# A linear-attention and channel-mix kernel: the layout of transposed q, where batch 0 is divided, and a new order of the work

## The chip, the cores and the metric

One core of one Trainium2 chip runs the whole program. The metric is device time in microseconds (us) of one execution; a verdict compares medians of several executions. A core has TensorE (matmuls, PE in the profile; PEld is its loading of weights), VectorE (DVE), ScalarE (ACT), GpSimd (POOL) and SyncE (SP). POOL and SP issue the DMAs here.

## What is computed

There are 8 batches, 8 heads, 576 tokens and 64 values a head; the model width C is 512 and the hidden width F is 1024. The reference, cut to its core:

```python
kv  = einsum('bhsd,bhse->bhde', k, v)             # 64x64 per head, no softmax
out = einsum('bhsd,bhde->bhse', q, kv)            # called u below
out = out / sqrt(mean(out*out, -1) + 1e-6) * g_norm
x   = out with the heads side by side: (8, 576, 512)
xp  = x moved down by one token (zero first)
xk  = mu_k*x + (1-mu_k)*xp;  xr = mu_r*x + (1-mu_r)*xp
kk  = maximum(xk @ w_k, 0);  vv = (kk*kk) @ w_v;  r = 1/(1+exp(-(xr @ w_r)))
result = r * vv
```

## The kernel before

**Attention, by batch.** q, k and v come in as bf16, by DMAs that POOL issues (in the order of the `ld` pieces); of batch 0, half of k and of v come as fp32 by SP (`ldh`) and are cast on the chip (`cst`). With the heads in two groups z = 0 and 1, the pieces of batch b are, by name and line:
- `kv` (L265): the 64x64 products of k and v, 72 matmuls for all heads; `kc` copies them from PSUM, `ks` (L271) parts even and odd rows with a permutation matrix, `kd` copies them back to SBUF as `kv`.
- `tq` (L350): VectorE transposes q in blocks of 32x32 fp32 words, each word being two neighbouring bf16 values of a head. A partition of the loaded q holds 36 tokens (QJ) of 1/16 (QP) of a head, so a block turns one token of 32 partitions. Two pieces a batch (four for batch 0, which goes by head group), 18 in all. The result is `qT`: a partition holds a pair of the 64 values, and along it lie the tokens of two heads (e = 0 and 1), two bf16 (r = 0 and 1) each. Word number: 36 times the source partition plus the token in it, so that tokens lie in their order and a transpose writes words 36 apart.
- `u` (L281): kv times qT. A piece covers half of the tokens (i = 0 or 1) of the heads. For r = 0, then r = 1, it runs one matmul for each pair of heads m and each e, of 32 rows and 64 columns; the eight of one r sit in different places of the array.
- `uc` (scale by g_norm, to SBUF), `sq` (squares), `ss` (a matmul that sums squares by head), `rs` (1/sqrt), `sp` (batches 2 and later: SP's DMAs spread rs over the partitions, L418), `mul`, `d` (difference to the token before, L298), `mk`/`mr` (times mu-1), `xk`/`xr` (sum, L311).

**Channel mix, by groups of 512 rows.** `k` (L494, group 0: L470) is xk times w_k in PSUM, `relu` (L453) and `ksq` (square, L504) bring it to SBUF, `r` (L516) and `sig` are the gate, `v` (L536) is the product with w_v, `out` (L549) multiplies it with the gate, `st` stores it. Group g needs batches g-1 and g; group 0's `k0.<half><i><z>` uses 256 rows of batch 0 and head group z.

**Batch 0** is cut more finely, by head group and by token parts: columns 0 to 256 and 256 to 576 (`PARTS`, with GA = 256), while the other batches are cut at 288 (HS). In a name such as `xk0.01`, the last digits are head group and part.

**PSUM** holds four tiles `ps` of two banks each. A piece that takes a tile waits until the readers of its last content are done.

**The order.** Nothing is scheduled by a program: the string `ORDER` lists all pieces, and each engine runs its own in that order, so an engine that waits holds up all that it has behind. `@A` and `@D` put a piece that can run on either on ScalarE or VectorE. `z:512` is a matmul on zeros that fills TensorE before k0.000; its result is overwritten.

Of the kernel before, what the change touches and what calls it, by code (L numbers as in the profile page):

```python
# [7 lines left out]
FP32 = mybir.dt.float32  # L8
BF16 = mybir.dt.bfloat16
# [47 lines left out]
def kernel(  # L57
# [13 lines left out]
    nc = tc.nc  # L71

    B, H, S, HD = q.shape
# [5 lines left out]
    NZ = NHP // 2  # L79
    HS = S // 2  # L80
    QP = 16
# [9 lines left out]

    const = ctx.enter_context(tc.tile_pool(name="const", bufs=1))
    sb = ctx.enter_context(tc.tile_pool(name="sb", bufs=2))
    psum = ctx.enter_context(tc.tile_pool(name="psum", bufs=2, space=bass.MemoryType.PSUM))
    ctx.enter_context(tc.manual_schedule())

    BUFS = {
        "k": (3, (128, NHP, NJ * HD), BF16),
        "v": (3, (128, NHP, NJ * HD), BF16),
        "q": (3, (128, QJ * HD), BF16),  # L100
        "kv": (2, (128, 2, 2 * HD), BF16),
        "kvn": (2, (128, 2, 2 * HD), BF16),
        "qT": (2, (128, 2 * S, 2), BF16),
        "uT": (4, (128, 2, S), BF16),
        "sq": (3, (128, 2, S), BF16),
        "rs": (3, (128, 2, S), BF16),
        "rsc": (1, (128, S), BF16),
        "d": (2, (128, 2, S), BF16),
        "md": (4, (128, 2, S), BF16),
        "sqk": (2, (128, NFC, G), BF16),  # L110
        "relu": (3, (128, 2, G), BF16),
        "sig": (3, (128, 2, C), BF16),
        "out": (3, (128, 2, C), FP32),
        "ps": (4, (128, 2, 512), FP32),
    }
# [158 lines left out]
    def u_tiles(pss, kv, qT, zs, c0, c1):  # L274
        for r in range(2):
            for z in zs:
                for y in range(2):
                    for e in range(2):
                        m = 2 * z + y
                        rows_ = slice(32 * m, 32 * m + 32)  # L280
                        nc.tensor.matmul(pss[z][64 * e:64 * e + 64, y, 0:c1 - c0], kv[rows_, r, HD * e:HD * e + HD],  # L281
                                         qT[rows_, S * e + c0:S * e + c1, r], start=(r == 0), stop=(r == 1))
# [9 lines left out]
    def blends(b, z, name, x0, w, deps, mds, dd):  # L292
# [9 lines left out]
        for key, dst, m0 in (("k", xk, 0), ("r", xr, NHP)):  # L302
            md = mds[key]

            def mul(eng, md=md, m0=m0):
                for y in range(2):
                    hp = m0 + 2 * z + y
                    scale(eng, get(md)[:, y, cs], dd.t[:, y, cs], cols[:, hp:hp + 1])

            def plus(_, md=md, dst=dst):  # L310
                nc.vector.tensor_tensor(out=dst[:, 2 * z:2 * z + 2, r0:r0 + w], in0=md.t[:, :, cs], in1=xT[:, :, cur],  # L311
                                        op=ALU.add)

            m = add(f"m{key}" + name, "DA", mul, deps=[df, p_cols], bufs=[dd, md])
            done[key] = add(f"x{key}" + name, "D", plus, deps=[m] + x_free.get((b - RB, key), []),
                            bufs=[md, x_buf[(b, z)]])
        return done

    PARTS = ((0, GA), (GA, S))

    def parts(b):
        return PARTS if b == 0 else ((0, HS), (HS, S))

    def attention(b):
        kin, vin, qin = (kvq[(m, b)] for m in ("k", "v", "q"))
        kv, qT = Buf("kv"), Buf("qT")
        bufs = [{t: Buf(t) for t in ("uT", "sq", "rs", "d")} for z in range(NZ)]
        mds = [{"k": Buf("md"), "r": Buf("md")} for z in range(NZ)]
        x_ready[b] = {"k": [], "r": []}
        zss = [[0], [1]] if b == 0 else [[0, 1]]  # L330
        qd, kvcs = {}, {}
        for zs in zss:
# [12 lines left out]
            for i in range(2):  # L345
                def tq(_, i=i, part=part):
                    src = qin.t.bitcast(FP32).rearrange("q (j i) -> q j i", i=32)
                    dst = get(qT).rearrange("q t r -> q (t r)").bitcast(FP32).rearrange("q (p j) -> q j p", j=QJ)
                    js = slice(QJ // 2 * i, QJ // 2 * i + QJ // 2)
                    nc.vector.transpose(out=dst[part, js, :], in_=src[part, js, :])  # L350

                ts.append(add(f"tq{name}.{i}", "D", tq, deps=sum((loaded[("q", b, z)] for z in zs), []), bufs=[qin, qT]))
# [4 lines left out]
        for i, (c0, c1) in enumerate(parts(b)):  # L357
            for zs in zss:
                p = add(f"u{b}." + "".join(map(str, zs)) + f".{i}", "T", lambda _, zs=zs, i=i, c0=c0, c1=c1: u_tiles(
                    {z: get(us[z][i]) for z in zs}, kv.t, qT.t, zs, c0, c1),  # L360
                    deps=sum(([*qd[z], kvcs[z]] for z in zs), []), bufs=[us[z][i] for z in zs] + [qT, kv])
                for z in zs:
                    pu[(z, i)] = p
        secs = {}
        for z in range(NZ):
            for i, (c0, c1) in enumerate(parts(b)):
                name, ps, w, cs = f"{b}.{z}{i}", us[z][i], c1 - c0, slice(c0, c1)
                uT, sq = bufs[z]["uT"], bufs[z]["sq"]
                uc = add("uc" + name, "DA", lambda eng, ps=ps, uT=uT, cs=cs, w=w: scale(
# [235 lines left out]
```

## Time and profile before

| | us |
|---|---|
| median of 3 runs | 202.54 (202.31 to 202.99) |
| the profiled execution | 202.8 |
| its span, first to last instruction | 201.0 |
| TensorE busy in the span | 189.8 |
| VectorE busy | 138.3 |
| ScalarE busy | 129.5 |
| the 18 transposes, together | 21.3 |

The span is the part of the execution that has instructions in it; 1.8 us of the execution lie around it. Busy times of engines overlap. The granted clock of TensorE is 1.00 over the whole span. A busy TensorE includes the fillers, 37 of which are recorded with 12.4 us.

### The profile page before, as it was taken

The page shows a single profiled execution, that of the slowest core. Times are in us where ns is not written, and L with a number is a line of the kernel's source. Part 1 is how long each engine was busy: PE and PEld are TensorE (multiplying, and loading weights), DVE is VectorE, ACT ScalarE, POOL GpSimd, SP SyncE. Part 2 cuts the span into 40 slices and gives each one's busy share as a digit, 9 for nine tenths or more (in the row PEclk, how much of TensorE's full clock was granted, in tenths as well). Part 3 has the DMA queues.
Part 4 walks back from the last instruction along what each step waited for, and adds up shares of the span by engine and source line. Part 5 has one row for each costly group of instructions (what it writes and reads, how often), then busy time and mean ns, then how long its engine had stood idle before and what let it go on. Part 6 is the DMA issues. An engine that isn't in the chain of part 4 may idle for free.

```text
span 201.0 us, 4245 instructions
## 1 busy us (share of the span) xinstructions
PE 189.8 (94%) x1743; PEld 93.9 (47%) x1765; DVE 138.3 (69%) x229; ACT 129.5 (64%) x172; POOL 23.1 (12%) x41
## 2 busy tenths in 40 slices
PE   7999779988999999999999999999999999999992
PEld 2545664443544444544545754444444444444451
DVE  1596687997879999797897798998454423133252
ACT  2367978957998579898968689375963554312500
POOL 7743331212100500000000000000000000000000
PEclk9999999999999999999999999999999999999999
DMA  6999999999999999999614242551000202045044
GB/s 212 198 210 216 201 206 216 203 207 219 207 230 257 246 250 265 238 213 194 230 26 94 105 124 50 165 163 57 0 0 0 104 3 104 0 157 209 0 151 166
DMA packets 21016, 30.63 MB, mean 152 GB/s; under 512 B 1917, under 2 KB 14469, under 8 KB 20997
## 3 DMA queue, kind: packets, MB, share of 16 engines
q0 software_dynamic: 11264, 16.19, 45.1%
q1 hardware_dynamic: 9588, 14.03, 21.9%
q8 instruction: 14, 0.23, 0.4%
q10 hardware_dynamic: 144, 0.13, 0.2%
q14 instruction: 6, 0.04, 0.1%
HBM read 33.56 MB, written 9.44 MB: 214 GB/s over the span
## 4 chain that ended last, share of the span: by engine, by line
PE 73%; DMA 9%; DVE 8%; ACT 4%; issue 2%; POOL 2%; SPq 1%; POOLq 0%; DVEq 0%
PE ps L536 27%; PE ps L494 26%; PE ps L516 12%; DMA w_k<-in_moe_w_k_dram 6%; DMA rs<-rsc 3%; PE ps L281 2%; DVE out L549 2%; DVE qT L350 2%; PE ps L470 1%; PE ps L265 1%; ACT relu L453 1%; ACT md L134 1%; DVE xk L311 1%; SPq L418 1%; PE ps L380 1%
## 5 line engine op out<-in xcount | busy, mean ns | idle before, releaser
L536 PE MATMUL ps<-w_v,sqk 128*128 128x512 bf16 (+1 forms) x286 | 65.8, 373 | 0.8 <-issue 0.3
L494 PE MATMUL ps<-xk,w_k 128*128 128x512 bf16 (+1 forms) x282 | 58.2, 355 | 0.7 <-issue 0.3
L453 ACT ACTIVATE relu<-ps 128x1024 bf16<-128x1024 f32 x36 | 36.2, 1022 | 27.9 <-PE ps L494 27.5
L536 PEld LDWEIGHTS <-sqk 128*128 128x128 bf16 x296 | 28.0, 98 | 32.8 <-issue 2.4
L494 PEld LDWEIGHTS <-w_k 128*128 128x128 bf16 x288 | 27.7, 98 | 27.5 <-issue 1.5
L504 DVE TENSOR_TENSOR sqk<-relu 128x1024 bf16<-128x1024 bf16 x32 | 21.6, 687 | 21.5 <-ACT relu L453 21.4
L516 PE MATMUL ps<-w_r,xr 128*128 128x512 bf16 x140 | 33.2, 379 | 0.2
L549 DVE TENSOR_TENSOR out<-ps,sig 128x1024 f32<-128x1024 f32 x16 | 19.5, 1220 | 11.5 <-PE ps L536 7.3
L371 ACT ACTIVATE sq<-ps 128x576 bf16<-128x576 f32 (+2 forms) x32 | 20.3, 650 | 9.1 <-PE ps L281 8.0
L526 ACT ACTIVATE sig<-ps 128x1024 bf16<-128x1024 f32 x18 | 18.3, 1022 | 8.5 <-PE ps L516 7.8
L350 DVE STREAM_TRANSPOSE qT<-q 128x576 f32<-128x576 f32 (+1 forms) x18 | 21.3, 1201 | 2.5 <-DMA q<-in_q_dram 2.1
L516 PEld LDWEIGHTS <-xr 128*128 128x128 bf16 x144 | 13.9, 98 | 16.6 <-issue 0.5
L134 ACT ACTIVATE md<-d,cols 128x576 bf16<-128x576 bf16 (+2 forms) x26 | 16.7, 698 | 0.5 <-DVE d L298 0.5
L144 ACT ACT_TABLE_LOAD x12 | 15.4, 1283 | 0.9 <-PEq L589 0.7
L136 DVE TENSOR_SCALAR uT<-ps,cols 128x576 bf16<-128x576 f32 (+1 forms) x16 | 12.5, 801 | 4.4 <-PE ps L281 2.2
L393 DVE TENSOR_TENSOR xT<-uT,rs 128x1152 bf16<-128x1152 bf16 (+2 forms) x18 | 12.3, 685 | 3.6 <-ACT rs L286 3.5
L311 DVE TENSOR_TENSOR xk<-md,xT 128x1152 bf16<-128x1152 bf16 (+2 forms) x18 | 12.2, 687 | 3.4 <-ACT md L134 3.2
L136 DVE TENSOR_SCALAR md<-d,cols 128x576 bf16<-128x576 bf16 (+2 forms) x46 | 13.9, 354 | 0.2
L438 PE MATMUL ps<-zero 128*128 128x512 bf16 x37 | 12.4, 477 | 1.5 <-DVE zero L164 1.2
L298 DVE TENSOR_TENSOR d<-xT 128x1152 bf16<-128x1152 bf16 (+2 forms) x18 | 12.5, 692 | 0.5
L311 DVE TENSOR_TENSOR xr<-md,xT 128x1152 bf16<-128x1152 bf16 (+2 forms) x18 | 12.1, 683 | 0.7 <-ACT md L134 0.6
L134 ACT ACTIVATE uT<-ps,cols 128x576 bf16<-128x576 f32 (+2 forms) x16 | 11.9, 743 | 0.6 <-PE ps L281 0.6
(47 smaller groups left out, 105.9 us busy)
## 6 DMA issues: line engine op xcount, KB each, us to landing
out_dram<-out SPq DMA_DIRECT2D x35, 256.0 KB, 2.4
q<-in_q_dram POOLq DMA_DIRECT2D x7, 576.0 KB, 21.4
v<-in_v_dram POOLq DMA_DIRECT2D x6, 576.0 KB, 21.9
k<-in_k_dram POOLq DMA_DIRECT2D x6, 576.0 KB, 20.5
rs<-rsc SPq DMA_DIRECT2D x48, 72.0 KB, 2.8
w_k<-in_moe_w_k_dram POOLq DMA_DIRECT2D x2, 512.0 KB, 11.3
w_v<-in_moe_w_v_dram POOLq DMA_DIRECT2D x2, 512.0 KB, 16.1
k<-in_k_dram POOLq DMA_DIRECT2D x3, 288.0 KB, 12.8
```

The source lines that it names most:

```text
L134: nc.scalar.mul(out=dst, in_=src, mul=col)
L136: nc.vector.tensor_scalar(out=dst, in0=src, scalar1=col, scalar2=None, op0=ALU.mult)
L311: nc.vector.tensor_tensor(out=dst[:, 2 * z:2 * z + 2, r0:r0 + w], in0=md.t[:, :, cs], in1=xT[:, :, cur], op=ALU.add)
L350: nc.vector.transpose(out=dst[part, js, :], in_=src[part, js, :])
L371: sq_ = add("sq" + name, "A", lambda _, ps=ps, sq=sq, cs=cs, w=w: nc.scalar.activation(out=get(sq)[:, :, cs], in_=ps.t[:, :, 0:w], func=AF ...
L453: nc.scalar.activation(out=get(rt), in_=ps.t, func=AF.Relu)
L494: nc.tensor.matmul(get(ps)[:, fc % 2, a0:a1], w_k_sb[:, cc, 128 * fc:128 * fc + 128], xk[:, cc, x0:x0 + a1 - a0], start=(cc == 0), stop=(c ...
L504: nc.vector.tensor_mul(out=get(sqk)[:, 2 * f2:2 * f2 + 2, :], in0=rt.t, in1=rt.t)
L516: nc.tensor.matmul(get(ps)[:, ci % 2, :], xr[:, cc, n0:n0 + 128], w_r_sb[:, cc, :], start=(cc == 0), stop=(cc == NHP - 1))
L526: nc.scalar.activation(out=get(sg), in_=ps.t, func=AF.Sigmoid)
L536: nc.tensor.matmul(get(ps)[:, bank, cs], sqk.t[:, fc, 128 * ci:128 * ci + 128], w_v_sb[:, fc, cs], start=(fc == 0), stop=(fc == NFC - 1))
L549: dv = add(f"out{g}.{c2}", "D", lambda _, ps=ps, sg=sg, ot=ot: nc.vector.tensor_mul(out=get(ot), in0=ps.t, in1=sg.t), deps=ms + [sg_done], ...
```

## The change

It has four parts.
1. `qT` gets another layout. The token of a partition is written as 2a + b, and the word number is 64a + 2p + b, where p is the partition's place in its block. A transpose then writes words two apart (8 bytes) instead of 36 apart (144 bytes). The same number of words is written by the same 18 instructions.
2. `u` reads its moving operand in token order out of that layout: for each p, for each a, the two words b = 0 and 1 beside each other, then a step of 64 words. It takes one of every two bf16 values, as before. A half of the tokens is now eight values of p, which is 288 tokens.
3. For that reason batch 0 is divided at 288 columns like the others. The second half of group 0 (rows 256 to 512) then needs both parts, and its dependencies say so.
4. `ORDER` is another one: the same pieces in another sequence, with 42 `z:512` instead of 38. On VectorE instead of ScalarE now run 13 instead of 16 of the 32 `uc`, 15 instead of 13 `mk` and 11 instead of 10 `mr` of 18 each, 5 instead of 2 `kc` and 2 instead of 0 `kd` of 9 each, and 3 instead of 2 of the 4 `cst`.

The diff. The two orders are shown from their start to the first u piece of batch 2, broken into lines, with a run of n `z:512` written as `z:512*n`; the rest of both is left out.

```diff
-ldh.v ldh.k table seta setp perm ld.q0.0 ld.q0.1 ident ld.k0.1 ld.v0.1 ld.wk1 ld.wk0 ld.k1.0 ld.q1.01 ld.v1.0
-ld.v1.1 ld.k1.1 ld.wv0 ld.wv1 ld.wr ld.q2.01 ld.v2.01 ld.k2.01 zz cst.v0@D cst.k1@A small setb cst.v1@D
-tq0.0.1 tq0.0.0 cst.k0@A z:512*17 kv0.0 tr9 cols kc0.0@A ks0.0 kd0.0@A z:512*5 u0.0.0 sq0.00 u0.0.1 tq0.1.1
-uc0.01@A uc0.00@D z:512*2 ss0.00 rs0.00 tq0.1.0 z:512*2 kv0.1 ld.k3.01 ld.v3.01 ld.q3.01 kc0.1@A sq0.01
-z:512*2 ks0.1 kd0.1@A z:512*2 u0.1.1 u0.1.0 sq0.10 uc0.10@A z:512*3 ss0.10 rs0.10 mul0.00 d0.00 mk0.00@D
-xk0.00 mr0.00@D z:512*1 ss0.01 rs0.01 z:512*4 k0.000 mul0.10 d0.10 sq0.11 ss0.11 mk0.10@D uc0.11@A mul0.01
-xk0.10 k0.001 rs0.11 d0.01 mul0.11 d0.11 mk0.01@A mk0.11@A xk0.11 k0.010 xk0.01 tq1.01.1 relu0.00 k0.011
-xr0.00 k0.110 k0.111 mr0.11@A xr0.11 relu0.01 ksq0.01 ksq0.00 relu0.11 tq1.01.0 ld.q4.01 k0.100 k0.101
-mr0.10@A kv1.01 ld.v4.01 ld.k4.01 relu0.10 ksq0.11 ksq0.10 kc1.01@A ks1.01 kd1.01@A u1.01.1 uc1.11@A uc1.01@D
-sq1.11 mr0.01@D v0.3.0 xr0.01 u1.01.0 uc1.10@D v0.2.0 sq1.00 uc1.00@D v0.3.1 sq1.01 xr0.10 ss1.0 sq1.10 ss1.3
-ss1.1 rs1.0 rs1.1 mul1.0 v0.2.1 d1.0 rs1.3 ss1.2 rs1.2 r0.0 r0.1 sig0.0 r0.2 mul1.1 d1.1 mk1.1@D mr1.1@D xk1.1
-tq2.01.1 r0.3 v0.0.0 v0.0.1 mk1.0@A v0.1.0 xk1.0 v0.1.1 mr1.0@A sig0.1 out0.0 k1.4 kv2.01 ld.k5.01 kc2.01@A
-ks2.01 kd2.01@A tq2.01.0 ld.q5.01 ld.v5.01 u2.01.1
...
+ldh.v ldh.k ld.q0.0 ld.q0.1 ld.v0.1 ld.k0.1 ld.v1.0 seta zz setb setp ident perm ld.wk0 ld.k1.1 ld.wk1 ld.v1.1
+ld.k1.0 ld.q1.01 ld.wv0 ld.wv1 ld.wr ld.k2.01 ld.v2.01 ld.q2.01 table cst.v1@D cst.v0@A cst.k0@D cst.k1@D
+z:512*16 kv0.0 kc0.0@A z:512*2 ks0.0 tq0.0.0 tq0.0.1 tq0.1.0 small z:512*2 tr9 cols kd0.0@A u0.0.1 uc0.01@A
+sq0.01 tq0.1.1 z:512*1 u0.0.0 sq0.00 z:512*7 kv0.1 ld.v3.01 ld.k3.01 ld.q3.01 uc0.00@D kc0.1@A ss0.01 ss0.00
+rs0.01 ks0.1 mul0.01 kd0.1@A rs0.00 mul0.00 z:512*3 u0.1.1 uc0.11@D sq0.11 u0.1.0 sq0.10 z:512*11 ss0.10
+uc0.10@A d0.00 mk0.00@D xk0.00 k0.000 k0.010 d0.01 mr0.01@D mk0.01@D xk0.01 ss0.11 rs0.10 mul0.10 d0.10
+mr0.10@A k0.110 mk0.10@D xk0.10 k0.001 k0.011 rs0.11 mul0.11 relu0.00 d0.11 mk0.11@A xk0.11 ksq0.00 kv1.01
+ld.k4.01 ld.v4.01 kc1.01@D mr0.00@D mr0.11@A relu0.01 k0.100 k0.101 relu0.10 tq1.01.1 tq1.01.0 ks1.01 kd1.01@A
+ksq0.01 k0.111 relu0.11 u1.01.0 uc1.10@A ksq0.10 sq1.10 uc1.00@D u1.01.1 sq1.11 ksq0.11 uc1.11@A sq1.00 v0.0.0
+v0.1.0 xr0.00 xr0.10 ss1.2 sq1.01 rs1.2 ss1.3 rs1.3 v0.0.1 uc1.01@D ss1.0 v0.1.1 mul1.1 ss1.1 rs1.1 r0.0 r0.1
+rs1.0 xr0.01 xr0.11 r0.2 mul1.0 d1.0 r0.3 d1.1 sig0.0 mk1.0@D xk1.0 sig0.1 out0.0 v0.2.0 v0.3.0 v0.3.1 v0.2.1
+mk1.1@A xk1.1 mr1.0@A kv2.01 ld.k6.01 kc2.01@A out0.1 k1.4 ks2.01 kd2.01@A tq2.01.0 tq2.01.1 k1.5 relu1.2
+u2.01.0
...
         "q": (3, (128, QJ * HD), BF16),
         "kv": (2, (128, 2, 2 * HD), BF16),
         "kvn": (2, (128, 2, 2 * HD), BF16),
-        "qT": (2, (128, 2 * S, 2), BF16),
+        "qT": (2, (128, QJ // 2, 2 * QP, 2, 2), BF16),
         "uT": (4, (128, 2, S), BF16),
         "sq": (3, (128, 2, S), BF16),
         "rs": (3, (128, 2, S), BF16),
                 nc.tensor.matmul(ps[part, r, 256:256 + 2 * HD], perm[part, r, f, part], kvn[part, :, HD * f:HD * f + HD],
                                  start=(f == 0), stop=(f == 1))
 
-    def u_tiles(pss, kv, qT, zs, c0, c1):
+    def u_tiles(pss, kv, qT, zs, i):
         for r in range(2):
             for z in zs:
                 for y in range(2):
                     for e in range(2):
                         m = 2 * z + y
                         rows_ = slice(32 * m, 32 * m + 32)
-                        nc.tensor.matmul(pss[z][64 * e:64 * e + 64, y, 0:c1 - c0], kv[rows_, r, HD * e:HD * e + HD],
-                                         qT[rows_, S * e + c0:S * e + c1, r], start=(r == 0), stop=(r == 1))
+                        p0 = QP * e + QP // 2 * i
+                        nc.tensor.matmul(pss[z][64 * e:64 * e + 64, y, 0:HS], kv[rows_, r, HD * e:HD * e + HD],
+                                         qT[rows_, :, p0:p0 + QP // 2, :, r].rearrange("q a p b -> q p a b"),
+                                         start=(r == 0), stop=(r == 1))
 
     def rms(_, dst, ps):
         table(RSQRT)
                             bufs=[md, x_buf[(b, z)]])
         return done
 
-    PARTS = ((0, GA), (GA, S))
-
-    def parts(b):
-        return PARTS if b == 0 else ((0, HS), (HS, S))
+    PARTS = ((0, HS), (HS, S))
 
     def attention(b):
         kin, vin, qin = (kvq[(m, b)] for m in ("k", "v", "q"))
             ts = []
             for i in range(2):
                 def tq(_, i=i, part=part):
-                    src = qin.t.bitcast(FP32).rearrange("q (j i) -> q j i", i=32)
-                    dst = get(qT).rearrange("q t r -> q (t r)").bitcast(FP32).rearrange("q (p j) -> q j p", j=QJ)
-                    js = slice(QJ // 2 * i, QJ // 2 * i + QJ // 2)
-                    nc.vector.transpose(out=dst[part, js, :], in_=src[part, js, :])
+                    src = qin.t.bitcast(FP32).rearrange("q (a b i) -> q a b i", b=2, i=32)
+                    dst = get(qT).rearrange("q a p b r -> q (a p b r)").bitcast(FP32).rearrange("q (a p b) -> q a b p", p=32, b=2)
+                    js = slice(QJ // 4 * i, QJ // 4 * i + QJ // 4)
+                    nc.vector.transpose(out=dst[part, js], in_=src[part, js])
 
                 ts.append(add(f"tq{name}.{i}", "D", tq, deps=sum((loaded[("q", b, z)] for z in zs), []), bufs=[qin, qT]))
             for z in zs:
                 qd[z], kvcs[z] = ts, c
         us = [[Buf("ps") for i in range(2)] for z in range(NZ)]
         pu = {}
-        for i, (c0, c1) in enumerate(parts(b)):
+        for i in range(2):
             for zs in zss:
-                p = add(f"u{b}." + "".join(map(str, zs)) + f".{i}", "T", lambda _, zs=zs, i=i, c0=c0, c1=c1: u_tiles(
-                    {z: get(us[z][i]) for z in zs}, kv.t, qT.t, zs, c0, c1),
+                p = add(f"u{b}." + "".join(map(str, zs)) + f".{i}", "T", lambda _, zs=zs, i=i: u_tiles(
+                    {z: get(us[z][i]) for z in zs}, kv.t, qT.t, zs, i),
                     deps=sum(([*qd[z], kvcs[z]] for z in zs), []), bufs=[us[z][i] for z in zs] + [qT, kv])
                 for z in zs:
                     pu[(z, i)] = p
         secs = {}
         for z in range(NZ):
-            for i, (c0, c1) in enumerate(parts(b)):
+            for i, (c0, c1) in enumerate(PARTS):
                 name, ps, w, cs = f"{b}.{z}{i}", us[z][i], c1 - c0, slice(c0, c1)
                 uT, sq = bufs[z]["uT"], bufs[z]["sq"]
                 uc = add("uc" + name, "DA", lambda eng, ps=ps, uT=uT, cs=cs, w=w: scale(
                                                      w_k_sb[:, hp, 128 * fc:128 * fc + 128], xk[:, hp, GA * half:GA * half + GA],
                                                      start=(hp == 0 and fc % 2 == 0), stop=(hp == NHP - 1 and fc % 2 == 1))
 
-                        m = add(f"k0.{half}{i}{z}", "T", k_part, deps=[x_ready[0]["k"][2 * z + half], p_wk[z], m],
+                        m = add(f"k0.{half}{i}{z}", "T", k_part, deps=x_ready[0]["k"][2 * z:2 * z + half + 1] + [p_wk[z], m],
                                 bufs=[ps])
                     k_all.append(m)
                     a = add(f"relu0.{half}{i}", "A", lambda _, ps=ps, rt=rt: k_relu(_, ps, rt), deps=[m], bufs=[ps, rt])
                         nc.tensor.matmul(get(ps)[:, ci % 2, :], xr[:, cc, n0:n0 + 128], w_r_sb[:, cc, :],
                                          start=(cc == 0), stop=(cc == NHP - 1))
 
-                deps = need["r"] if g else [x_ready[0]["r"][2 * z + c2] for z in range(NZ)]
+                deps = need["r"] if g else [x for z in range(NZ) for x in x_ready[0]["r"][2 * z:2 * z + c2 + 1]]
                 m = add(f"r{g}.{2 * c2 + x}", "T", r_mm, deps=[m] if m else deps + ([p_wr] if g == 0 else []), bufs=[ps])
                 if x:
                     r_all.append(m)

```

## The prediction

> **What bounds the kernel now.** I read the page's busy line first, then the table of stages, then who ended TensorE's waits, then the rows of the two operations that change.
>
> The page, busy time and share of the span:
> ```profile
> PE 189.8 (94%) x1743; PEld 93.9 (47%) x1765; DVE 138.3 (69%) x229; ACT 129.5 (64%) x172; POOL 23.1 (12%) x41
> ```
> TensorE (PE) is busy 94% of 201.0 us; VectorE (DVE), which does the transposes, 69%. The table of stages (start:end, length, then busy us by engine) says where this average holds:
> ```profile
> 0.00:18.57 18.57, 16.57 (x157) 7.55 (x160) 10.38 (x32) 9.19 (x16) 10.23 (x22) 1.00 0.99 208
> 18.57:28.00 9.43, 8.29 (x138) 6.88 (x138) 7.75 (x17) 8.81 (x15) 4.25 (x6) 1.00 1.18 207
> 28.00:36.00 8.00, 6.61 (x85) 3.26 (x72) 5.29 (x11) 6.04 (x11) 1.84 (x3) 1.00 1.18 209
> 36.00:47.50 11.50, 10.09 (x130) 4.96 (x131) 10.45 (x16) 8.13 (x13) 2.78 (x4) 1.00 1.21 209
> 47.50:68.00 20.50, 19.94 (x289) 9.27 (x290) 17.55 (x28) 18.24 (x25) 2.77 (x4) 1.00 1.13 233
> 68.00:94.00 26.00, 25.74 (x252) 11.64 (x254) 22.74 (x33) 21.76 (x29) 1.28 (x2) 1.00 1.13 237
> 94.00:130.00 36.00, 35.74 (x411) 19.34 (x415) 31.50 (x53) 26.86 (x36) 0.00 (x0) 1.00 0.40 115
> 130.00:188.00 58.00, 57.74 (x266) 26.32 (x269) 28.43 (x42) 29.48 (x32) 0.00 (x0) 1.00 0.20 70
> ```
> Up to 18.57 TensorE is kept busy with filler matmuls (z) while batch 0 is prepared. From 18.57 (k0.000) to 47.5 it idles 1.14 + 1.39 + 1.41 = 3.9 us. From 47.5 to 188 it idles 1.3 us in 140.5, although VectorE is 86 to 88% busy up to 130. So the time is: when k0.000 starts, what TensorE loses up to 47, a full TensorE, a tail of 3.8 us. Who ended TensorE's waits between 18 and 47:
> ```profile
> PE ps L271 <- ACT kvn L128: 1.2, 2, 0.7
> PE ps L470 <- DVE xk L311: 1.1, 1, 1.1
> PE ps L281 <- ACT kv L128: 0.9, 2, 0.5
> PE ps L281 <- DVE out L549: 0.3, 1, 0.3
> PE ps L281 <- ACT sq L371: 0.2, 1, 0.2
> ```
> None of them is a transpose: they are the steps kv, kc, ks, kd, u, which the old order runs with nothing between, and the blend of batch 0. A shorter transpose by itself therefore gives at most what the new order makes of it. The rows that change, and two that price them (groups by shape: busy us, mean ns):
> ```profile
> L350 DVE STREAM_TRANSPOSE qT<-q 128x576 f32<-128x576 f32 x14 | 16.7, 1203 | 0.4 <-PE ps L281 0.4
> L350 DVE STREAM_TRANSPOSE qT<-q 64x576 f32<-64x576 f32 x4 | 4.6, 1193 | 2.2 <-DMA q<-in_q_dram 2.1
> L281 PE MATMUL ps<-qT,kv 32*64 32x288 bf16 x224 | 7.0, 297 | 1.4 <-ACT kv L128 0.9 <-DVE out L549 0.3 <-ACT sq L371 0.2
> L549 DVE TENSOR_TENSOR out<-ps,sig 128x1024 f32<-128x1024 f32 x16 | 19.5, 1220 | 11.5 <-PE ps L536 7.3 <-ACT sig L526 3.6 <-DMA out_dram<-out 0.7
> L563 DVE TENSOR_TENSOR out<-ps,sig 128x512 f32<-128x512 f32 x3 | 2.1, 688 | 4.8 <-PE ps L536 4.8
> ```
>
> **The transposes.** L549 and L563 differ by 512 fp32 elements and 532 ns: 1.04 ns an element and 155 ns fixed. A transpose has 576, so 754 ns at that rate; it takes 1202, which is 1.82 ns an element. Its writes go 36 words (144 bytes) apart. No row shows a transpose with close writes: the cost is between 754 and 1202 ns; a loss is excluded, since the count of words stays and only the step shrinks. I take 0.76, the rate of the nearest fp32 rows. That is 18 x 0.44 = 8 us less on VectorE, off the path wherever TensorE is full. The Trainium skill, "Advanced Engine Details and Errata", section "SBUF Cachelines", says that SBUF lines are 16 bytes and that an access pattern needs two hits on a line for full speed; by it the old writes (one hit) pay and the new ones (8 bytes apart, two hits) do not, and u with two hits instead of four stays free, which is the sum forecast here.
>
> **u.** One u piece of both head groups is two rounds of eight matmuls; in the trace the eight start 3 to 4 ns apart, the second round 130 ns later, and the next work 0.39 us behind the first. Two of the eight (e = 0 and 1) read the same 32 partitions at the same time. Before, each read words 4 bytes apart; after, pairs of words, then a step of 256 bytes. No row shows such a read. Lower end 0: same columns, nothing shortens. Upper end by the nearest row for scattered access, the old transpose: 1.82 / 1.04 = 1.75 times, 130 to 228 ns a round, 2 x 98 = 0.2 us a piece. I take 0, the nearest row being u itself, and keep the other end as a rival.
>
> **The start, walked in the new order** with durations of this profile (us from the span's start). One filler fewer ahead of kv0.0, and VectorE instead of ScalarE (ACT) casts k by 7.0: kv0.0 at 7.9 (8.14 before). kc0.0 starts 0.8 behind it, ks0.0 at 9.1, two fillers, tr9, cols at 10.4 to 10.6 (VectorE has done three transposes by then). ScalarE: uc0.01 to 11.4, sq0.01 and sq0.00 (0.65 each) to 12.7. Seven fillers hold kv0.1 to 13.1; kc0.1 to 14.3, rs0.01 to 15.0, kd0.1 to 15.4, rs0.00 to 16.1. VectorE: mul0.00 to 16.6, uc0.11 0.75, then d, mk, xk of part 00 (0.45 + 0.5 + 0.45) to 18.8. So **k0.000 at 18.85, 0.3 later than now**; the last 11 fillers end about then too. w_k no longer decides: its first half lands near 17.0 (the load ahead of it is now 1.2 us shorter than the other w_k half; now both are in at 18.53). POOL issues q first and perm later, so loads may land up to 1 us earlier still; nothing on this path uses that.
>
> From there: d, mr, mk, xk of part 01 end at 20.7, in time for k0.110 (20.95 to 21.85). mul, d, mk, xk of 10 end at 22.55: k0.001 waits 0.75. kv1.01 (loads in by 24.2) runs to 25.2, k0.100 to 26.1. ScalarE is now the full one: relu0.00 to 24.7, mk0.11 25.75, mr0.11 26.8, relu0.01 27.8, relu0.10 28.8, kd1.01 29.2, relu0.11 30.2, uc1.10 30.95, sq1.10 31.6. VectorE: xk0.11 26.25, ksq0.00 26.95, kc1.01 27.35, mr0.00 27.85, two transposes to 29.4. TensorE: k0.101 waits 0.1, ks1.01 0.3, k0.111 to 28.5, u1.01.0 at 29.45 (waits 0.95 for the transposes, 1.8 at their old length), u1.01.1 waits 0.4 for relu0.11's PSUM tile, v0.0.0 waits 1.0 for that of sq1.10 (31.65). Then v0 (4 x 0.86), ss1 (4 x 0.25), r0 (3.45), v0 (3.45) run through to 43.0; w_v and w_r (31.7 and 34.2 now) are in. kv2.01 0.75, k1.4, ks2.01, k1.5 to 45.8, transposes of batch 2 to 45.9, u2.01.0 done at 46.4. In the trace u2.01.1 is done at 46.55 **without k1.5**. So the new order is ahead by 0.15 + 0.86 = 1.0; about 0.3 goes for the 0.09 us that TensorE loses at each change of matmul tiling, of which my walk counts only some. **Gain 0.7 us.**
>
> Behind 47 the pieces are the same in both orders (171.0 us from k0.000 at 0.216 us a 512-column matmul), with 46 changes of tiling in each, so what is ahead stays ahead if no wait comes up. The thinnest cover is group 2's: from ss2 to the first k2 piece lie 15.6 us of TensorE work now and 15.5 after; now the spread of rs through SP (8 DMAs, 52.5 to 62.9) and the blend behind it end at 66.36, and k2.4 waits a little (67.54). uc goes from 16 to 13 on VectorE and blends and casts come to it (+4.6 - 2.4 us), so with the transposes it has some 6 us less, ScalarE some 4 us less. The tail (v8.3, out, store) is unchanged.
>
> **Sum**: +0.3 at the start, -1.0 up to 47, 0 behind: span 200.3 instead of 201.0, 202.1 for the profiled execution (202.8, 1.8 of it outside the span). Against the median of 202.54 this is **201.8 us**.
>
> **Rivals.** (1) *u pays for its scattered read.* For: four matmuls of two streams share each partition, and a round at 130 ns is already the streaming time of 288 columns, with no slack; against: no row. 12 pieces of batches 2 to 7 lie on a full TensorE: 12 x 0.2 = 2.4 us, so 204.2; at twice the round 3.1, so 204.9. It decides from 0.7 / 24 = 29 ns more a round. The Trainium skill, "SBUF — State Buffer", section "Who interferes with whom", gives TensorE one SBUF read port for the moving operand; by that rule two streams with half the hits each would share one port, and this rival holds. The trace so far shows two streams at full rate, with four hits a line. (2) *The transposes stay at 1.2 us*, the step not being what slows them: u1.01.0 at 30.3, v0.0.0 0.55 later, u2.01.0 0.9 later: 203.2. (3) *The new order waits less than my walk says*, because PSUM tiles are handed on earlier than I take them (1.4 us of waits) : 200.4. (4) *Group 2 waits for the spread*: 0.7 us, which takes the gain: 202.5.
>
> **Numbers.** The forecast's mechanism, short transposes and a free u, with (3) and (4) inside it: 0.56, split 0.38 faster, 0.15 same, 0.03 slower. Rival (1): 0.32, split 0.01, 0.03, 0.28. Rival (2): 0.12, split 0.02, 0.03, 0.07. Faster, same and slower are parted at 0.3% (0.6 us), about what a measurement of this kernel can tell: 0.41, 0.21, 0.38. Range 200.0 (below (3)) to 204.8 (near the upper end of (1)). The forecast's own range is 200.0 to 202.9.
>
> **What would show it.** L350 near 760 ns, else (2). Rounds of u 130 ns apart and 0.39 us a piece, else (1). k0.000 near 18.85; TensorE waiting for xk, then for qT, relu and sq between 21 and 32; u2 done by 46.4; under 1.5 us idle from 47.5 to the last v8. An idle TensorE ahead of the first k2 piece would be (4). The forecast is wrong if u lengthens, or if the new order opens waits behind 47.

## The result

| | before | after |
|---|---|---|
| median (4 executions each) | 202.60 us (202.31 to 202.99) | 204.59 us (204.37 to 205.07) |
| ratio after / before | | 1.0100 [1.0075, 1.0125] |
| the profiled execution, its span | 202.8, 201.0 | 204.55, 202.8 |
| k0.000 starts | 18.57 | 19.26 |
| the last v matmul starts | 196.88 | 198.54 |
| the 18 transposes, together | 21.3 | 13.2 |
| u, from the last start of one round to the first of the next | 130 ns | 211 ns |

The kernel is 2.0 us slower where 0.7 us faster was forecast. (In some executions of the kernels below that have the new order, TensorE's granted clock falls to 0.50 for some 3 us; where a median mixes such executions with others, the times at full clock are given apart.)

The busy line of the page of after:

```profile
PE 195.3 (96%) x1769; PEld 93.8 (46%) x1769; DVE 134.5 (66%) x238; ACT 125.1 (62%) x163; POOL 23.3 (11%) x41
```

VectorE and ScalarE have 3.8 and 4.4 us less than before, and TensorE has 5.5 us more (189.8 before), though it computes the same with four fillers more (4 x 0.22 = 0.9 us). Of the 5.5 us, 1.8 are no work: the page of before has 1743 matmul rows (PE) for 1765 weight loads (PEld), that of after 1769 for 1769. The 22 rows that before's trace lacks show as holes of 0.05 or 0.16 us, and these holes make 1.8 us. The table of stages (start:end, length, then busy us of PE, PEld, DVE, ACT, POOL):

```profile
18.50:28.00 9.50, 9.16 (x147) 7.53 (x145) 7.22 (x20) 7.46 (x13) 3.08 (x5) 1.00 1.15 202
28.00:36.00 8.00, 6.55 (x62) 3.22 (x61) 6.23 (x12) 6.67 (x12) 2.02 (x3) 1.00 1.22 204
36.00:47.50 11.50, 11.50 (x139) 5.18 (x136) 9.31 (x14) 9.72 (x14) 0.74 (x1) 1.00 1.17 212
47.50:68.00 20.50, 20.50 (x288) 9.08 (x288) 15.94 (x27) 17.87 (x23) 5.41 (x8) 1.00 1.15 232
68.00:94.00 26.00, 25.48 (x290) 11.52 (x289) 19.93 (x33) 18.20 (x23) 0.55 (x1) 1.00 1.07 220
```

From 18.5 to 47.5 TensorE idles 0.34 + 1.45 + 0 = 1.8 us. Before, the table has 3.9 us there, 0.3 of them holes of missing rows. So the new order does fill holes up to 47. From 47.5 to 188 it idles 0.52 (all between 68 and 94). The 1.3 us that the table has for before in that stretch are missing rows but for one wait of 0.2, the last line in the list of before's waits behind 47 (the four of its "issue" lines are holes of missing rows):

```profile
PE ps L494 <- issue: 0.3, 2, 0.2
PE ps L536 <- issue: 0.3, 2, 0.2
PE ps L494 <- DVE out L549: 0.2, 1, 0.2
```

So behind 47 there was next to nothing to fill. TensorE idles less than before, and the time is longer all the same: what grew is busy time. The groups by shape (busy us, mean ns of one) say of which instruction:

```profile
L282 PE MATMUL ps<-qT,kv 32*64 32x288 bf16 x256 | 12.1, 412 | 0.6 <-DVE qT L349 0.6
L349 DVE STREAM_TRANSPOSE qT<-q 128x576 f32<-128x576 f32 x14 | 10.2, 759 | 0.0
L349 DVE STREAM_TRANSPOSE qT<-q 64x576 f32<-64x576 f32 x4 | 3.0, 762 | 0.1
```

The transposes went from 1203 to 759 ns. A u matmul went from 297 to 412 ns. The timeline of TensorE shows what that does to a piece (start, length, line, count):

```profile
45.19 0.68 PE L282 MATMUL ps<-qT,kv 32*64 32x288 bf16 x16
45.79 1.90 PE L493 MATMUL ps<-xk,w_k 128*128 128x512 bf16 x8
```

The sixteen matmuls of u2.01.0 start at 45.19, and the next work starts 0.61 us behind; before, it came 0.39 us behind. Fourteen such pieces of both head groups and four of one make up u, and the four are longer by 0.22 us each as well. The list of who ended TensorE's waits, behind k0.000:

```profile
PE ps L535 <- ACT sq L370: 0.9, 1, 0.9
PE ps L282 <- DVE qT L349: 0.6, 1, 0.6
PE ps L493 <- DVE out L548: 0.4, 1, 0.4
PE ps L469 <- DVE xk L313: 0.3, 1, 0.3
```

These are the waits that the walk of the new order forecast between 21 and 32 (xk, qT, a PSUM tile held by sq), and one for `out` at 71. None is a wait that could explain 2 us.

### The profile page after: what moved, and what is told of

It reads as the page before. It is cut to its first block, busy times and chain, and to the rows that moved or that the text cites. A ratio compares the mean times of both kernels' runs of the same rounds, so it can differ in the third digit from the quotient of the medians.

```text
span 202.8 us, 4282 instructions
## 1 busy us (share of the span) xinstructions
PE 195.3 (96%) x1769; PEld 93.8 (46%) x1769; DVE 134.5 (66%) x238; ACT 125.1 (62%) x163; POOL 23.3 (11%) x41
## 4 chain that ended last, share of the span: by engine, by line
PE 75%; DMA 8%; DVE 8%; ACT 6%; SPq 1%; issue 1%; ACTq 0%
PE ps L535 26%; PE ps L493 23%; PE ps L515 13%; DMA out_dram<-out 5%; PE ps L437 5%; PE ps L282 4%; DMA rs<-rsc 3%; PE ps L265 2%; DVE md L136 1%; DVE qT L349 1%; ACT L144 1%; ACT relu L452 1%; DVE xk L313 1%; ACT sq L370 1%; DVE uT L136 1%; ACT rs L288 1%
## 5 line engine op out<-in xcount | busy, mean ns | idle before, releaser
L503 DVE TENSOR_TENSOR sqk<-relu 128x1024 bf16<-128x1024 bf16 x32 | 21.3, 685 | 12.6 <-ACT relu L452 12.6
L525 ACT ACTIVATE sig<-ps 128x1024 bf16<-128x1024 f32 x18 | 18.1, 1021 | 13.4 <-PE ps L515 13.2
L370 ACT ACTIVATE sq<-ps 128x576 bf16<-128x576 f32 x32 | 19.9, 652 | 6.4 <-PE ps L282 4.3
L392 DVE TENSOR_TENSOR xT<-uT,rs 128x1152 bf16<-128x1152 bf16 (+1 forms) x18 | 12.3, 684 | 6.9 <-ACT rs L288 4.5
L136 DVE TENSOR_SCALAR md<-d,cols 128x576 bf16<-128x576 bf16 (+1 forms) x52 | 15.7, 351 | 0.4
L134 ACT ACTIVATE uT<-ps,cols 128x576 bf16<-128x576 f32 x19 | 13.6, 745 | 2.0 <-PE ps L282 2.0
L136 DVE TENSOR_SCALAR uT<-ps,cols 128x576 bf16<-128x576 f32 x13 | 10.4, 815 | 6.4 <-ACT sq L370 3.6
L437 PE MATMUL ps<-zero 128*128 128x512 bf16 x43 | 13.2, 455 | 1.2 <-DVE zero L164 1.2
L134 ACT ACTIVATE md<-d,cols 128x576 bf16<-128x576 bf16 (+1 forms) x20 | 12.7, 700 | 1.4 <-DVE d L300 1.4
L313 DVE TENSOR_TENSOR xk<-md,xT 128x1152 bf16<-128x1152 bf16 (+1 forms) x18 | 12.3, 688 | 1.8 <-ACT md L134 1.4
L313 DVE TENSOR_TENSOR xr<-md,xT 128x1152 bf16<-128x1152 bf16 (+1 forms) x18 | 12.0, 686 | 2.1 <-ACT md L134 2.0
L349 DVE STREAM_TRANSPOSE qT<-q 128x576 f32<-128x576 f32 (+1 forms) x18 | 13.2, 760 | 0.1
L300 DVE TENSOR_TENSOR d<-xT 128x1152 bf16<-128x1152 bf16 (+1 forms) x18 | 12.4, 692 | 0.4
```

What stands on the lines that cost most here:

```text
L134: nc.scalar.mul(out=dst, in_=src, mul=col)
L136: nc.vector.tensor_scalar(out=dst, in0=src, scalar1=col, scalar2=None, op0=ALU.mult)
L370: sq_ = add("sq" + name, "A", lambda _, ps=ps, sq=sq, cs=cs, w=w: nc.scalar.activation(out=get(sq)[:, :, cs], in_=ps.t[:, :, 0:w], func=AF ...
L437: nc.tensor.matmul(get(k_ps[(0, 0)])[:, 0, 0:n], zero[:, 0:128], zero[:, 0:n], start=not started, stop=not started)
L503: nc.vector.tensor_mul(out=get(sqk)[:, 2 * f2:2 * f2 + 2, :], in0=rt.t, in1=rt.t)
L525: nc.scalar.activation(out=get(sg), in_=ps.t, func=AF.Sigmoid)
```

## The experiments

The theories of the first four runs, written before them. **A**: the u matmuls are slow because two streams (e = 0 and 1) read the same 32 partitions through one read port, and pairs of words leave each stream half of what it needs. **B**: one stream by itself is slow when it reads pairs. (Experiments 5 and 6 then ask what of it counts: how many 16-byte lines it touches, or how often it jumps.) **C**: the new order costs the time, whatever u does. Below, a line is 16 bytes of one partition, which is four words of qT, and a line that is left and come back to counts again. The **round** of a kernel is taken where u runs four rounds back to back (u0.1.1 and u0.1.0, ahead of k0.000): from the first start of a round to that of the next, from the second round on. In after it is 245 ns; 288 columns at the rate of the 512-column matmuls (216 ns) would take 121. (The expectations use a looser round: about 130 ns for the free read and 230 to 237 for that of after.)

### 1. u reads along the layout: u_layout_order

```diff
-qT[rows_, :, p0:p0 + QP // 2, :, r].rearrange("q a p b -> q p a b"),
+qT[rows_, :, p0:p0 + QP // 2, :, r],
```

> The changed kernel, but u reads its moving operand in the order in which it lies (16 words in a row, four on each 16 bytes), so the tokens of its output come in another order than the reference's; all else is unchanged. If the scattered read is the whole loss: a round of eight u matmuls goes back from 237 to about 130 ns, a piece from 0.61 to 0.39 us, and 12 pieces on a full TensorE give 2.6 us: 204.6 becomes 202.0, and 0.6 us under the kernel before remain as what the new order and the short transposes earn. If the loss comes from the new order, rounds may shorten, but the time stays above 203.5.

Median 202.01 us, ratio 0.9954 [0.9926, 0.9983]; span 200.4. Its group and its timeline:

```profile
L282 PE MATMUL ps<-qT,kv 32*64 32x288 bf16 x256 | 8.1, 291 | 0.6 <-DVE qT L349 0.6
```

```profile
44.46 0.45 PE L282 MATMUL ps<-qT,kv 32*64 32x288 bf16 x16
44.84 1.47 PE L493 MATMUL ps<-xk,w_k 128*128 128x512 bf16 x6
```

Same data, same layout, same count of columns, same order of the work, and only the sequence in which u reads them differs: a round is 125 ns, a piece 0.38 us, and 2.6 us of the median are gone. C falls, and the read is the cause. That leaves A and B.

### 2. The same read, with the results put in order in PSUM: u_psum_order

```diff
-nc.tensor.matmul(pss[z][64 * e:64 * e + 64, y, 0:HS], kv[rows_, r, HD * e:HD * e + HD],
-                 qT[rows_, :, p0:p0 + QP // 2, :, r].rearrange("q a p b -> q p a b"),
+nc.tensor.matmul(pss[z][64 * e:64 * e + 64, y, 0:HS].rearrange("q (p a b) -> q a p b", a=QJ // 2, b=2),
+                 kv[rows_, r, HD * e:HD * e + HD], qT[rows_, :, p0:p0 + QP // 2, :, r],
```

> The same read in the order in which it lies, with the results written to PSUM at their token's place, two beside each other and then a step of 36, so that the output is in token order again. If only the SBUF side of u is slow, rounds of 130 ns and 202.0 us. If PSUM writes two by two cost what SBUF reads two by two cost, rounds stay near 237 ns and the time at 204.6.

Median 202.14 us, ratio 0.9964 [0.9934, 0.9994]; span 200.4, round 123 ns. Writing PSUM two fp32 values at a time, with a jump behind each pair, cost nothing, so this computes what after computes at the price of experiment 1. Its u2.01.0 is done at 45.0. What became of that lead is in the list of waits between 47 and 188, and in the timeline around the longer one:

```profile
PE ps L493 <- DVE out L548: 0.6, 1, 0.6
PE ps L493 <- DVE xk L313: 0.2, 1, 0.2
```

```profile
69.35 1.23 DVE L548 TENSOR_TENSOR out<-ps,sig 128x1024 f32<-128x1024 f32 x1 [2.31 <-DMA out_dram<-out]
...
70.63 1.24 PE L493 MATMUL ps<-xk,w_k 128*128 128x512 bf16 x5 [0.58 <-DVE out L548]
```

VectorE waits 2.31 us for a store to release one of the three `out` tiles, and TensorE then waits 0.58 us for the PSUM tile that this `out` reads. Taken from the starts of the matmuls, the gaps of this kind between 60 and 80 make 1.6 us here, and 0.85 us in after, which comes there later.

### 3 and 4. One stream, by pairs and singly: one_stream_pairs, one_stream_singles

```diff
-for e in range(2):
+for e in range(1):
...
-nc.tensor.matmul(pss[z][64 * e:64 * e + 64, y, 0:HS], kv[rows_, r, HD * e:HD * e + HD],
+nc.tensor.matmul(pss[z][:, y, 0:HS], kv[rows_, r, :],
```

The second of the two also reads `"q a p b -> q p b a"`, which takes one word of a line at a time.

> One u matmul of 32 rows and 128 columns for both e, with the moving operand of e = 0 alone (the second head of each pair gets the first one's tokens, the other half of qT is not read): one stream a partition instead of two, still read two by two. Theory A, that the two streams of a partition share one read of a 16-byte line about every 0.83 ns: a round of four takes about 130 ns. Theory B, that each stream alone is slowed by reading two by two: about 237 ns.

> As one_stream_pairs (tokens of e = 0 alone), but every value read lies 256 bytes from the one before, one on a line; the token order is another one than the reference's. Theory A: 288 lines at 0.83 ns, a round of about 240 ns. Theory B: twice the time of pairs, about 470 ns.

The groups, first of pairs, then of singles:

```profile
L282 PE MATMUL ps<-qT,kv 32*128 32x288 bf16 x128 | 12.0, 408 | 0.6 <-DVE qT L349 0.6
```

```profile
L282 PE MATMUL ps<-qT,kv 32*128 32x288 bf16 x128 | 20.5, 649 | 0.6 <-DVE qT L349 0.6
```

One stream per 32 partitions, reading pairs: a round of 246 ns, against 245 ns with two streams. Read singly: 486 ns. (The two were executed once, with 206.75 and 214.07 us; the rounds are the measurement.) **A falls**: with one stream there is nothing to share, and the read is as slow. B holds, and it has a size: 288 lines take 486 ns and 144 lines 245, so 1.7 ns a line. That is the time of four columns at full rate (4 x 216 / 512 = 1.69 ns): four columns to a line are enough, and a line with two or with one takes as long. Three to a line, or more than four, were not measured.

### 5 and 6. Lines or jumps: two_streams_fours, even_stride_pairs

The first reads runs of four words, each in one line, with a jump behind every run. The second reads no jumps but every second word, so that a line is left after two hits.

```diff
-qT[rows_, :, p0:p0 + QP // 2, :, r].rearrange("q a p b -> q p a b"),
+qT[rows_, :, p0:p0 + QP // 2, :, r].rearrange("q a (s t) b -> q s a (t b)", t=2),
```

```diff
-qT[rows_, :, p0:p0 + QP // 2, :, r].rearrange("q a p b -> q p a b"),
+qT[rows_, :, QP * e:QP * e + QP, i, r],
```

> The changed kernel with u's moving operand read four words in a row (two neighbouring p, two b), then a step of 256 bytes; the token order is another one than the reference's. A row of four fills one 16-byte line. If what counts is lines (72 a stream, 1.6 ns each by the runs before: 117 ns), a round takes about 130 ns. If what counts is jumps (pairs: 143 jumps cost 97 ns more than the streaming time, 0.7 ns each), 71 jumps give about 180 ns.

> The changed kernel with u reading every second word, 8 bytes apart and even over 16 values at a time (tokens of one parity a piece, in another order than the reference's): two values on each 16-byte line, but no jump inside a row of 16. Lines: 144 a stream, about 230 ns a round as with pairs. Jumps: 17, about 130 to 140 ns.

The groups, first of fours, then of the even stride:

```profile
L282 PE MATMUL ps<-qT,kv 32*64 32x288 bf16 x256 | 8.1, 291 | 0.6 <-DVE qT L349 0.6
```

```profile
L282 PE MATMUL ps<-qT,kv 32*64 32x288 bf16 x256 | 12.0, 412 | 0.8 <-DVE qT L349 0.8
```

72 jumps and 72 lines: 124 ns a round, free. 144 lines without the jumps of after: 244 to 247 ns a round, and the 412 ns of after again. So it is the number of lines, and a jump of 256 bytes costs nothing. The two runs also bear out the 16 bytes: with lines of 8 bytes the fours would have touched 144, with lines of 32 the even stride 72, and neither took the time of that. (Executed once each, with 203.16 and 204.43 us. The first is not near 202 because its k0.000 came at 19.49; see the start, below.)

### 7. Words four apart: words_four_apart

Can the layout give u its runs of four in token order? Then a transpose writes words 16 bytes apart.

```diff
-"qT": (2, (128, QJ // 2, 2 * QP, 2, 2), BF16),
+"qT": (2, (128, QJ // 4, 2 * QP, 4, 2), BF16),
...
-js = slice(QJ // 4 * i, QJ // 4 * i + QJ // 4)
+js = slice(5 * i, 5 + 4 * i)
```

> qT with four tokens beside each other: the transposes write words four apart (16 bytes, one on a line), u reads in token order four words in a row. The output is the reference's. By lines, u is free again (130 ns a round) and the transposes pay again: if one write a line is what made them slow, 1.2 us as in the kernel before; if only far steps are slow, 0.76 us.

```profile
L349 DVE STREAM_TRANSPOSE qT<-q 128x640 f32<-128x640 f32 x7 | 9.2, 1317 | 0.0
L349 DVE STREAM_TRANSPOSE qT<-q 128x512 f32<-128x512 f32 x7 | 7.6, 1085 | 0.0
```

The two sizes differ by 128 words and 232 ns: 1.81 ns a word. At 144 bytes apart it was 1.82 and at 8 bytes apart it is 1.05, both with the 155 ns that the prediction takes as fixed from the `out` rows; with these 155 ns the two rows above come to 1.82 each. So a write 16 bytes from the last costs as much as one 144 bytes away, and the step of 8 bytes is the widest of those tried that is cheap. u's rounds, with jumps of 512 bytes instead of the 256 of two_streams_fours, were 130 to 139 ns, but TensorE waited 2.6 us for qT, and the execution took 207.4 us. A token order that suits both engines is not to be had from the layout alone; experiment 2 has it by leaving the reordering to PSUM.

### 8 and 9. Order and layout parted: old_layout_new_order, new_layout_old_order

The first has before's layout and u (with 288 columns in batch 0) and the new ORDER; the second has the kernel of experiment 2 with the old ORDER. As diffs, the first against after, the second against u_psum_order:

```diff
-"qT": (2, (128, QJ // 2, 2 * QP, 2, 2), BF16),
+"qT": (2, (128, 2 * S, 2), BF16),
...
-qT[rows_, :, p0:p0 + QP // 2, :, r].rearrange("q a p b -> q p a b"),
+qT[rows_, S * e + c0:S * e + c1, r], start=(r == 0), stop=(r == 1))
...
-src = qin.t.bitcast(FP32).rearrange("q (a b i) -> q a b i", b=2, i=32)
+src = qin.t.bitcast(FP32).rearrange("q (j i) -> q j i", i=32)
...
```

```diff
-ldh.v ldh.k ld.q0.0 ld.q0.1 ld.v0.1 ld.k0.1 ld.v1.0 seta zz setb setp ident perm ld.wk0
...
+ldh.v ldh.k table seta setp perm ld.q0.0 ld.q0.1 ident ld.k0.1 ld.v0.1 ld.wk1 ld.wk0
...
```

> The new order and batch 0 at 288 columns, with the layout of qT and the reading of u of the kernel before: the transposes take 1.2 us again, u 0.39 us. If the order alone earned the 0.6 us, about 202.0. By the walk of the prediction the order leans on the short transposes (u1.01.0 and u2.01.0 wait for them): then 202.7 to 203.4, not faster than the kernel before.

> The order of the kernel before with the new layout, batch 0 at 288 columns, and u reading in the order in which it lies and writing PSUM at the token's place (0.39 us a piece). Only the transposes are shorter (8 us on VectorE) for an order that was not made for them. TensorE's waits in that order were for kv's chain and the blend, not for transposes: 202.2 to 202.7, 0 to 0.4 us faster than before. If the short transposes themselves carry the gain, 201.5.

old_layout_new_order: 205.88 us, ratio 1.0165 [1.0128, 1.0203] (at full clock 205.0 to 205.1, three executions). The waits that lead its list:

```profile
PE ps L281 <- DVE qT L350: 3.1, 5, 1.4
PE ps L536 <- ACT sq L371: 1.2, 1, 1.2
```

With transposes of 1191 ns the new order makes TensorE wait for qT five times. Rival (2) named the right wait and gave 203.2 us; by these executions it is 205.0.

new_layout_old_order: 201.94 us (201.65 to 202.31), ratio 0.9967 [0.9956, 0.9979], faster than before and than after. Its span is 200.1, k0.000 starts at 18.14 and the last v at 195.99. So short transposes with a free u earn 0.7 us without the new order.

### 10. The division at 288 by itself: old_cut_at_288

```diff
-PARTS = ((0, GA), (GA, S))
+PARTS = ((0, HS), (HS, S))
...
-m = add(f"k0.{half}{i}{z}", "T", k_part, deps=[x_ready[0]["k"][2 * z + half], p_wk[z], m],
+m = add(f"k0.{half}{i}{z}", "T", k_part, deps=x_ready[0]["k"][2 * z:2 * z + half + 1] + [p_wk[z], m],
...
```

> The kernel before with batch 0 divided at 288 columns and nothing else: old layout, old order, old reading. It parts what new_layout_old_order earned (0.7 us) between the division and the transposes. If the short transposes earn it, this one stays within 0.3 us of before (202.4 to 202.9); if the division does, about 202.0.

202.36 us, ratio 0.9994 [0.9984, 1.0004]: nothing that can be measured, and no more than 0.2%. So the division has at most a small part of new_layout_old_order's gain. By the two ratios some 0.5 us are left, give or take 0.3, for the transposes and for u, of which a piece takes 0.383 us there against 0.392 here (18 x 0.009 = 0.16 us). The list of waits of old_cut_at_288 between 18.5 and 48 shows two that new_layout_old_order doesn't have:

```profile
PE ps L281 <- DVE out L549: 0.3, 1, 0.3
PE ps L281 <- ACT sq L371: 0.2, 1, 0.2
```

The first is a PSUM tile that u waits for until VectorE has done an `out`. It starts that `out` at 44.09 here and at 43.80 in new_layout_old_order, behind a transpose of 1.19 us here and of 0.77 there. That this is the way of the gain is argued, not shown: the profiled execution of new_layout_old_order gives 0.4 us back in a wait for a load of k, and its last v starts only 0.2 us earlier than here (195.99 against 196.17).

### 11 and 12. A fourth `out` tile: psum_order_out4, out4_again

```diff
-"out": (3, (128, 2, C), FP32),
+"out": (4, (128, 2, C), FP32),
```

Both are u_psum_order with this line.

> u_psum_order with four buffers for out instead of three. In its trace a k2 piece waits 0.6 us for out1, which waits 2.3 us for a store of group 0 to land; a fourth buffer takes that wait away. If nothing else is late there: 0.5 us less than u_psum_order, about 201.5. If the time is set by what comes behind anyway, no change.

> psum_order_out4 once more, for its trace: with four buffers for out, no k2 piece waits for out (0.6 us in u_psum_order), u2.01.0 ends near 45.0 as in u_psum_order, the last v piece starts 0.6 to 1.4 us earlier than there (196.1), and the median is again 200.5 to 201.2. If the fourth buffer did not earn it, the waits stand elsewhere with the same sum and the time is near 202.

Medians 200.71 (ratio 0.9934 [0.9900, 0.9967]) and 202.22 us (0.9960 [0.9928, 0.9991]). At full clock the two agree better: 200.5 to 201.0 in eight executions and 200.8 to 201.6 in five, against 201.1 to 202.2 in six of u_psum_order, so about 1 us for the fourth tile. In the second one's list of waits `out` is gone, and the wait that TensorE has behind 47 is

```profile
PE ps L493 <- DVE xk L313: 0.6, 1, 0.6
```

in its place at 67. The gain rests on the times, not on this list: both executions profiled with four tiles had the clock cut, and out4_again starts u2.01.0 at 46.48, 1.8 us later than u_psum_order. That by itself may leave a store more time to land; in after, 0.55 us later than u_psum_order, the same wait is 0.4 instead of 0.6. At full clock this is the fastest version; in 10 of the 23 executions the clock was cut and they took 202.6 us or more. new_layout_old_order was never cut in its 12.

## Why the prediction was wrong

**The transposes: right.** 0.76 us forecast, 0.759 and 0.762 measured, out of the rate of the `out` rows. VectorE was forecast some 6 us less and ScalarE 4; they have 3.8 and 4.4. The transposes are 8.1 us less, so the pieces that came to VectorE added 4.3, where 2.2 were reckoned.

**u: the step that failed.** "I take 0, the nearest row being u itself." The step between rounds went from 130 to 211 ns (225 in the pieces of one head group), the last round of a piece got 0.13 us longer too, and a piece of both head groups went from 0.39 to 0.61 us. The row of u was nearest by name only: it showed u reading four words of each line, and the change took that away. The row that resembled the change was the other one in the same view, the transpose, an operation that already touched a new line with every word; it gave the upper end, 228 ns. That this came near is partly luck: it is the rate of one word to a line on VectorE, and TensorE's round with one word to a line takes 486. Rival (1), with 204.2 to 204.9 us, holds the measured 204.59. Its reason, two streams on one port, is refuted by experiment 3, and its size is luck too: it priced 12 pieces at 0.2, which is 2.4 us, where 18 pieces cost 0.22 each, 4.0 us, and 1.6 of these were absorbed. The Trainium skill, "SBUF — State Buffer", section "Who interferes with whom", gives TensorE one read port for the moving operand; no run here shows two streams slowing each other (245 ns a round for two, 246 for one). The Trainium skill, "Advanced Engine Details and Errata", section "SBUF Cachelines", asks for two hits on a line: VectorE's transposes agree (1.05 ns a word with two, 1.82 with one), and TensorE's moving operand does not (245 ns a round with two, 125 with four). That rule was cited for the forecast, and for TensorE the measurement decides against it.

**The start: u was left out.** k0.000 was forecast at 18.85 and came at 19.26. Where it comes scatters: four traces of the new order with a free u have it at 18.27, 18.49, 18.76 and 19.49 (u_layout_order, u_psum_order, out4_again, two_streams_fours), since the first u piece starts anywhere from 9.77 to 10.77 in them. From the start of that piece to k0.000 it is 8.5 to 8.7 us in these four, and 9.2 to 9.4 in the three that read by pairs (after, one_stream_pairs, even_stride_pairs). So the walk itself was within the scatter, and the four u pieces of batch 0, with 0.22 us more each, lie ahead of k0.000 on TensorE and put it off by 0.7; the prediction had counted them out, pricing the rival by 12 pieces of batches 2 to 7. One slip in the sum cost nothing: it sets +0.3 us for the start beside a lead of 1.0 us, but that lead is read at 46.4 us of the span and has the late start in it already. The walk's own deduction of 0.3 us for changes of tiling is what belongs there, and the total of 0.7 is the same.

**From k0.000 to u2.01.0: right in kind, too small.** Forecast 46.4 with k1.5 inside, 1.0 us ahead. Measured 45.8 in after, and 45.0 with a fast u, 1.6 and 2.4 us ahead. The waits were the forecast ones, and together shorter, 1.8 and 2.4 us by the tables and lists where the walk had 3.5: rival (3) in kind, though the wait for sq's tile, which it counted among those that go, stayed (0.9 and 1.0 us).

**"0 behind 47": wrong.** The 1.3 us of idle time that the prediction read there in before were missing rows but for 0.2, so the new order could win nothing and could lose. Two things were hidden in it. The first is how much of the slow u is paid. 18 pieces of u cost 18 x 0.22 = 4.0 us more in after than in u_psum_order, yet its span is only 2.4 us longer. The starts of the same pieces in the two traces show where the rest went: k0.000 is 0.8 us later in after, u2.01.0 starts 0.55 us later, and the last v 2.5 us later. So up to k0.000 0.1 of 0.9 us is absorbed. From there to u2.01.0 it is 0.7 us, since two more pieces would make it 1.2 and the waits of batch 1 are that much shorter. Behind it 0.8 of 12 x 0.22 = 2.7 us go, and the gaps between 60 and 80 are 0.8 us shorter in after. Together that is 1.6 us, the difference of 4.0 and 2.4.

The second is what the new order loses. Its lead over before is 2.4 us at 47 in u_psum_order, but the last v starts only 0.8 us earlier than before (196.09 against 196.88): 1.6 us are given back. The gaps between 60 and 80 have 1.3 of that (1.6 us against 0.35 in before, missing rows left aside); the rest was not located. Rival (4) named the place, and its 0.7 us was too little. The cover that the prediction reckoned in front of k2 was that of rs through SP; the longest of the waits was another, a store that had not landed and held `out`. Already in before the 0.2 us in front of k2.4 were a wait for `out`, as the list behind 47 has it; the blend had ended at 66.36, by the prediction's own reading, 1.2 us ahead.

**"A shorter transpose by itself gives at most what the new order makes of it": not borne out.** new_layout_old_order earned 0.7 us with the old order, some 0.5 of it not from the division, and with short transposes and a free u the new order earns no more than that, by medians. The sentence was read from who ended the waits, where no transpose stands. But a wait is put down to the last step of a queue: in old_cut_at_288, as in before, `out` and sq release u for 0.3 and 0.2 us, and VectorE reaches that `out` 0.3 us sooner with short transposes.

**The sum**, from the spans of the profiled executions:

| | us |
|---|---|
| before | 201.0 |
| short transposes, division, free u, in the old order (new_layout_old_order) | -0.9 |
| the new order on top of these (u_psum_order) | +0.3 |
| u by pairs in place of u along the layout (after) | +2.4 |
| after | 202.8 |

Single executions of one kernel differ by more than the first two terms can bear: u_psum_order at full clock took 201.1 to 202.2 us. By medians the first is -0.7 and the second between 0 and +0.2. The third is 2.4 by medians too (204.59 against 202.14).

## What to carry to other kernels

Count the 16-byte lines that a moving operand touches before you change a layout: four of the 4-byte steps to a line ran at full rate here, and half of that took twice the time for the same columns. Compare the counts of matmuls and of weight loads before you call a hole in TensorE's rows idle time: most of what seemed idle behind 47 in before was missing rows. A layout is shared by the engine that writes it and the one that reads it, so price the change on both, and look whether the reordering can go to a third place (here the PSUM write) that takes it for nothing. A faster piece of work is worth what the next resource behind it allows: a lead of 2.4 us was worth 0.8 until the output tiles were one more.

## What the runs showed of the hardware

- TensorE's moving read took 1.7 ns for each visit to a line of 16 bytes, with one stream or two, with jumps of 256 bytes or without: 288 columns in 288, 144 and 72 visits took 486, 245 and 125 ns a round, the last being about the streaming time. In words_four_apart, with 72 visits and jumps of 512 bytes, it was 130 to 139 ns; why was not followed up.
- A 32x32 transpose's write cost 1.05 ns a word at a step of 8 bytes and 1.81 to 1.82 ns at 16 and at 144 bytes.
- Matmul results written to PSUM in pairs of fp32 with jumps between cost nothing (123 ns a round in u_psum_order).
- TensorE's clock was cut in some executions of the new order, and of none of the 24 of new_layout_old_order and old_cut_at_288. The stretches of out4_again (after the busy times, the granted clock is the third figure from the end) show where:

```profile
28.00:29.00 1.00, 0.34 (x18) 0.30 (x21) 1.00 (x2) 1.00 (x2) 0.00 (x0) 1.00 1.17 177
29.00:30.00 1.00, 0.68 (x32) 0.24 (x12) 1.00 (x3) 0.91 (x3) 0.36 (x1) 1.00 1.22 202
30.00:31.00 1.00, 0.38 (x1) 0.19 (x2) 1.00 (x2) 1.00 (x4) 0.18 (x1) 0.98 1.25 208
31.00:32.00 1.00, 0.90 (x3) 0.35 (x3) 0.82 (x3) 1.00 (x3) 0.00 (x0) 0.50 1.23 205
```

It falls to 0.50 from 31 to 34, behind three us in which TensorE was busy for 1.4, waiting for qT and then for sq. words_four_apart, with longer waits there, shows a cut in the same stage (0.79 between 28 and 36). That the thin stretch brings the cut is only argued, and not by itself borne out: u_psum_order's trace has as thin a one (1.39 us busy from 28 to 31) and old_layout_new_order's a thinner one (0.99 us), and both kept their clock in these executions; one_stream_singles' clock is cut from 18.0 to 21.4, behind 11 us in which TensorE's rows leave no hole of 0.1 us. What decides it stays open.
